# Decode turns moved, unequal MoE steps per turn, six warm-up matmuls, masks added by VectorE in later units, and six units' exponentials and sums on ScalarE

## The chip, the core and the metric

The kernel runs on one core of one Trainium2 chip. The metric is the device time of one execution in microseconds (us), and a kernel is judged by the median of its runs. The core's engines each work through their own list of instructions in order: TensorE (PE, matmuls), VectorE (DVE), ScalarE (ACT), GpSimd (POOL), and SyncE (SP), which here only issues DMAs. They wait for each other by semaphores.

## The reference

```
scores = scale * q @ k.T                  # 4 batches, 8 heads, 576 positions, 64 dims
mask: local (0 <= i-j < 32) for heads 0..3, strided (i >= j, i % 32 == j % 32) for heads 4..7
attn  = exp(scores - max) / (sum + 1e-9)
x     = attn @ v                          # -> 2304 tokens x 512
x     = (sigmoid(x @ w_gate) * (x @ w_val)) @ w_out      # MoE 1, 1536 wide
out   = softplus(x @ w_in) @ w_out2                      # MoE 2, 2048 wide
```

## The kernel before

**Two kinds of work in one stream.** The attention is cut into 32 units (8 to a batch: a pair of heads and 4 to 6 pieces of the sequence; local units have pieces of 64 queries by 96 keys, strided units of 54 by 54). The MoE layers work on blocks of 512 tokens; each "step" of theirs is three 512-column matmuls, since every operand is split into a high and a low part (`mm3`, L67 to L69). The weights come as 64-bit words, and a "decode" of one piece (128x512, `decode_steps`) makes a high and a low part of it: two VectorE instructions (L108, L112), then L117 on VectorE, L121 on ScalarE, L122 and L125 on VectorE and L126 on GpSimd. While the attention runs, 12 pieces are decoded: 6 of weight group 0 (`w00`, `w01`, `w02`: gate, value and down weights), then 6 of group 1.

**The turn.** The attention is a hand-written pipeline in turns u = 0 to 34 (`stage`). In turn u the program issues `exponent(u-1)`, `scores(u)`, `values(u-3)`, loads, the first half of a decode if u is in `decode_at`, then `normalize(u-1)`, the second half of the decode, `outputs(u-3)` and `p_transposes(u-2)`. Between these parts the loop puts MoE steps from a generator (`filler`) and, in the first 9 turns, one `keep_busy` matmul on a constant (L372). The order is fixed: nothing is rescheduled, so an engine's list is the program's order.

**One unit's way.** `scores`: a mask matmul (identity by a mask table, L422) starts the PSUM bank `ps_s`, and the score matmuls add to it (L429). VectorE reduces the maximum out of `ps_s` (L435) and subtracts it into `sm` (L436); ScalarE takes one exponential over the whole of `sm` in the next turn (L443); VectorE sums (L451) and takes the reciprocal (L452); GpSimd multiplies (L453). In the turn after that, PE transposes `sm` into `ps_p` (L467) and ScalarE copies it to `pt` (L470). In the third turn PE multiplies `pt` by v into `ps_o` (L485), ScalarE rounds it to `xh` (L505), and VectorE takes the rest into `xl` (L506). There are two `ps_s` banks, and three banks for MoE results.

**Which turn does what.** Group 0 is decoded in turns 4, 5, 9, 10, 12 and 13, group 1 in turns 18 to 23. The first window of MoE steps (24: 8 for gates, 8 for values, 8 for the down projection of token block 0) puts 2 each into turns 7, 8 and 9; the other 18 are spread evenly over turns 11 to 18 (2, 2, 2, 3, 2, 2, 2, 3). `load_next` asks for the next raw weight piece on SP's queue: one ahead of the turns, others in turns 2, 5, 6 and 7, later ones behind each decode. After the attention the rest is MoE alone, ordered by `step`, `down` and `decode_next`.

Of the kernel before, what the change touches and what calls it, by code (L numbers as in the profile page):

```python
# [8 lines left out]
F32 = mybir.dt.float32  # L9
# [3 lines left out]
AF = mybir.ActivationFunctionType  # L13
ALU = mybir.AluOpType
AX = mybir.AxisListType
# [5 lines left out]
P = 128  # L21
# [11 lines left out]
HQ = 64  # L33
# [10 lines left out]
def tile_sparse_attention_moe_moe2(  # L44
# [10 lines left out]
    nc = tc.nc  # L55
    SCALE = 1.0 / float(D) ** 0.5
# [35 lines left out]
    def load_next():  # L92
        if todo:
            g, m, c = piece = todo.pop(0)
            src = w1[g, m] if g < NG1 else w2[g - NG1, m // 2]
            raw = rawp.tile([P, PIECE], U64, tag="raw", name="raw")
            nc.sync.dma_start(out=raw, in_=src[:, c * PIECE:(c + 1) * PIECE])
            raws[piece] = raw
            queue.append(piece)
# [181 lines left out]
    def attention():  # L281
        with ExitStack() as actx:
# [11 lines left out]
            pools = {  # L294
                "g": pool("gp", 1), "t": pool("tp", 2), "d": pool("decp", 1), "e": nc.vector,
                "hy": pool("ps_hy", 3, space=PSUM),
            }

            units = []
# [12 lines left out]
            qbuf = [const.tile([P, 2, QW], F32, name=f"qbuf{j}") for j in range(2)]  # L312

            def load(j, parts=1):
                b, hp, c0, cn = units[2 * j]
                loc, w, m = dims(2 * j)
                cn += units[2 * j + 1][3]
                qq = qbuf[j % 2]
                kk = qkp.tile([P, STRIDE + S], F32, tag="k", name="kt")
                k0, kn = (0, STRIDE + S) if loc else (STRIDE, cn * m)  # L320
                qn = (cn - 1) * m + HQ
                for i in range(parts):
                    for h in range(2):
                        r = slice(h * HQ, (h + 1) * HQ)
                        a, e = (0, units[0][3] * m, qn)[i:i + 2] if parts > 1 else (0, qn)
                        nc.sync.dma_start(out=qq[r, h, a:e], in_=q[b, hp][r, a:e])
                    a, e = (0, units[0][3] * m + w - m, kn)[i:i + 2] if parts > 1 else (0, kn)
                    (nc.scalar if j < 2 else nc.sync).dma_start(
                        out=kk[:, a:e], in_=k[b, hp][:, k0 + a:k0 + e]
                    )  # L330
                for i in (2 * j, 2 * j + 1):
                    qt[i], kt[i] = qq, kk

# [9 lines left out]
            load(1)  # L343
            load_v(0)
            load_v(1)
            load_next()
            load_v(2)

            scratch = acc[NBA - 1]
            ident = scratch[:, 0:P]  # L350
            make_identity(nc, ident)
            nc.vector.memset(qbuf[0][HQ:2 * HQ, 0, :], 0.0)
            nc.vector.memset(qbuf[0][0:HQ, 1, :], 0.0)

            one = const.tile([P, P], F32R, name="one")
            nc.vector.tensor_copy(one, ident)
# [5 lines left out]

            for t in sbuf:
                nc.vector.memset(t[:, :, LK:], 1e-9)
            for t in qbuf[1:]:
                nc.vector.memset(t[HQ:2 * HQ, 0, :], 0.0)
                nc.vector.memset(t[0:HQ, 1, :], 0.0)

            def keep_busy(n):
                ps = bank(pools, "y", "ps_w")  # L370
                for _ in range(n):
                    nc.tensor.matmul(ps, lhsT=one, rhs=idle, start=True, stop=True)  # L372
# [29 lines left out]
            def mask_runs(i):  # L402
                b, hp, c0, cn = units[i]
                if hp >= NLP:
                    return [(0, cn, m_str)]
                first, rest = m_loc[:, 0:LK], m_loc[:, LK:2 * LK]
                return [(0, 1, first), (1, cn, rest)] if c0 == 0 else [(0, cn, rest)]

            sm, pts, outs = {}, {}, {}

            def scores(i):
                b, hp, c0, cn = units[i]
                loc, w, m = dims(i)
                qq, kk = qt.pop(i), kt.pop(i)
                s = sbuf[i % 3][:, 0:cn, LK - w:LK]
                st = smp.tile([P, 2, 6], F32, tag="st", name="st")
                sm[i] = (s, sbuf[i % 3][:, 0:cn, LK - w:], st)
                ps = ps_s.tile([P, TB], F32, tag="s", name="ps_s")
                pv = ps[:, 0:cn * w].rearrange("p (c w) -> p c w", c=cn)
                runs = mask_runs(i)  # L420
                for j, (a0, a1, t) in enumerate(runs):
                    nc.tensor.matmul(  # L422
                        pv[:, a0:a1, :], lhsT=one,
                        rhs=t.unsqueeze(1).to_broadcast([P, a1 - a0, w]),
                        start=(j == 0), stop=False,
                    )
                for c in range(cn):
                    for h in range(2):
                        nc.tensor.matmul(  # L429
                            pv[h * HQ:(h + 1) * HQ, c, :],  # L430
                            lhsT=qq[:, h, (c0 + c) * m:(c0 + c) * m + HQ],
                            rhs=kk[:, (c0 + c) * m:(c0 + c) * m + w], start=False, stop=(c == cn - 1),
                        )
                top = st[:, 0, 0:cn]
                nc.vector.tensor_reduce(out=top, in_=pv, axis=AX.X, op=ALU.max)  # L435
                nc.vector.tensor_tensor(  # L436
                    out=s, in0=pv, in1=top.unsqueeze(2).to_broadcast([P, cn, w]), op=ALU.subtract
                )

            def exponent(i):  # L440
                m2 = 2 * HQ
                s = sm[i][0]
                nc.scalar.activation(out=s[:m2], in_=s[:m2], func=AF.Exp, scale=SCALE)  # L443

            def normalize(i):
                cn = units[i][3]
                loc, w, m = dims(i)
                m2 = 2 * HQ
                s, more, st = sm[i]
                r = st[:m2, 1, 0:cn]  # L450
                nc.vector.tensor_reduce(out=r, in_=more, axis=AX.X, op=ALU.add)  # L451
                nc.vector.reciprocal(r, r)  # L452
                nc.gpsimd.tensor_tensor(  # L453
                    out=s[:m2], in0=s[:m2], in1=r.unsqueeze(2).to_broadcast([m2, cn, w]),
                    op=ALU.mult,
                )
# [54 lines left out]
            PB = 2 * NPAIR  # L511
            START = PB + SKEW

            def stage(u):
                dec = decode_steps(pools, u >= PB) if u in decode_at else iter(())
                if 0 <= u - 1 < NU:
                    exponent(u - 1)
                if u < NU:
                    scores(u)
                if u % 2 and u + 3 < NU:  # L520
                    load((u + 3) // 2)
                if 0 <= u - 3 < NU:
                    values(u - 3)
                if 3 <= u < NU:
                    load_v(u)
                if u in (2, 5, 6, 7):
                    load_next()
                next(dec, None)
                yield
                if 0 <= u - 1 < NU:  # L530
                    normalize(u - 1)
                next(dec, None)
                if 0 <= u - 3 < NU:
                    outputs(u - 3)
                yield
                if 0 <= u - 2 < NU:
                    yield from p_transposes(u - 2)
# [11 lines left out]
                    yield from step((0, 2), (1, 2), pools)  # L549

            ahead = {START - 4: 2, START - 3: 2, START - 2: 2}
            units_of = [3 * GC * NCC, 8 * GC * NCC, 6 * GC * NCC]
            units_of[0] -= sum(ahead.values())
            filler = window(0)
            decode_at = (4, 5, 9, 10, 12, 13) + tuple(range(18, 24))
            keep_busy(3)
            for u in range(NU + SKEW):
                t, pos = divmod(u - START, PB)
                if t > 0 and pos == 0:
                    for _ in filler:  # L560
                        pass
                    filler = window(t)
                fill = ahead.get(u, 0)
                if t >= 0:
                    total = units_of[t]
                    fill = (pos + 1) * total // PB - pos * total // PB
                n = 0
                for j, _ in enumerate(stage(u)):
                    if u < START - 2 and j == 1:
                        keep_busy(1)  # L570
                    while n < fill * (j + 1) // 4:
                        n += 1
                        next(filler, None)
                while n < fill:
                    n += 1
                    next(filler, None)
# [3 lines left out]
    with tc.manual_schedule():  # L580
        attention()

        late = ctx.enter_context(tc.tile_pool(name="late", bufs=1))
# [9 lines left out]
        for i, cur in enumerate(rest):  # L593
            g, t = cur
# [91 lines left out]
```

## Time and profile before

| | us |
|---|---|
| median of 3 runs (949.97 to 950.58) | 950.56 |
| the profiled execution's own time | 950.28 |
| its span, first to last instruction | 948.5 |
| PE busy in the span | 931.4 |
| VectorE busy | 601.8 |
| ScalarE busy | 383.9 |
| GpSimd busy | 229.3 |

The span is what the trace shows; 1.8 us of the execution's time lie around it. PE is busy for 98% of the span, so a look at shares alone does not tell where time may be had: one has to look for the stretches in which PE waits, or runs at a lower granted clock.

### The profile page before, as it was taken

Reading aid. Unit: us, or ns where it says so; the run is one execution under the profiler, and the core shown is the slowest. Engines: PE = TensorE matmul, PEld = TensorE weight load, DVE = VectorE, ACT = ScalarE, POOL = GpSimd, SP = SyncE. Lnnn points to the kernel's source line nnn. Section 1 sums busy time; section 2 is a strip of 40 time slices with the busy share of each in tenths; the row PEclk is TensorE's granted clock in tenths of the full one; section 3 lists DMA queues with packets and bytes.
Section 4 is the critical chain, followed back from the end, with each engine's and each line's share of the span. In section 5 each row is a group of like instructions: output and inputs, shape, how many; then the busy total and the mean of one; then the engine's idle time right before and its main releaser. Section 6 shows DMA issues by size and latency. Waiting matters only on the chain.

```text
span 948.5 us, 13659 instructions
## 1 busy us (share of the span) xinstructions
PE 931.4 (98%) x5476; PEld 776.3 (82%) x5476; DVE 601.8 (63%) x979; ACT 383.9 (40%) x693; POOL 229.3 (24%) x194
## 2 busy tenths in 40 slices
PE   7889999999999999999999999999999999999998
PEld 5667888789888888888888887888888888888886
DVE  7787765337567367457555467676767685858554
ACT  2455545524122112112123355454545554545443
POOL 3232211004224023122125442221313040403000
PEclk9889999999999999999999999999999999999999
DMA  8655332002112011011110011110101020200022
GB/s 226 186 159 154 122 101 61 17 1 89 45 45 81 8 45 67 23 45 46 45 37 30 22 45 45 36 53 23 67 23 66 6 85 1 82 8 23 0 89 112
DMA packets 20688, 57.44 MB, mean 61 GB/s; under 512 B 2704, under 2 KB 3216, under 8 KB 20624
## 3 DMA queue, kind: packets, MB, share of 16 engines
q1 hardware_dynamic: 20192, 55.94, 18.3%
q8 instruction: 43, 0.70, 0.3%
q10 hardware_dynamic: 432, 0.62, 0.2%
q14 instruction: 21, 0.17, 0.1%
HBM read 51.83 MB, written 4.72 MB: 60 GB/s over the span
## 4 chain that ended last, share of the span: by engine, by line
PE 92%; DVE 5%; ACT 1%; POOL 1%; issue 1%; POOLq 0%; DVEq 0%
PE ps_y L67 12%; PE ps_y L69 12%; PE ps_y L68 12%; PE ps_h L69 7%; PE ps_h L68 7%; PE ps_h L67 7%; PE ps_g L67 5%; PE ps_g L68 5%; PE ps_g L69 5%; PE ps_v L67 5%; PE ps_v L69 5%; PE ps_v L68 5%; PE ps_s L429 2%; PE ps_o L485 2%; PE ps_p L467 1%; DVE f L112 1%
## 5 line engine op out<-in xcount | busy, mean ns | idle before, releaser
L156 ACT ACTIVATE gh<-sg 128x512 fp32r<-128x512 f32 (+1 forms) x140 | 82.5, 589 | 255.0 <-DVE sg L189 183.8
L157 DVE TENSOR_TENSOR gl<-sg,gh 128x512 fp32r<-128x512 f32 (+1 forms) x140 | 98.7, 705 | 50.2 <-ACT gh L156 46.6
L260 DVE TENSOR_TENSOR acc<-ps_y,acc 128x512 f32<-128x512 f32 x126 | 86.6, 688 | 68.4 <-PE ps_y L69 66.8
L209 DVE TENSOR_TENSOR acc<-ps_y,acc 128x512 f32<-128x512 f32 (+1 forms) x100 | 61.5, 634 | 68.7 <-PE ps_y L69 68.6
L240 DVE SCALAR_TENSOR_TENSOR sg<-ps_h,sg 128x512 f32<-128x512 f32 (+1 forms) x80 | 50.5, 632 | 37.2 <-ACT sg L233 37.1
L189 DVE TENSOR_TENSOR sg<-ps_v,sg 128x512 f32<-128x512 f32 (+1 forms) x60 | 38.2, 636 | 56.2 <-PE ps_v L69 56.1
L231 ACT ACTIVATE sg<-ps_h 128x512 f32<-128x512 f32 (+1 forms) x80 | 43.8, 548 | 61.2 <-PE ps_h L69 61.2
L112 DVE SCALAR_TENSOR_TENSOR f<-raw,f 128x512 uint32<-128x512 uint32 x68 | 66.4, 977 | 2.3
L125 POOL TENSOR_TENSOR f<-f,w00h 128x512 f32<-128x512 f32 x12 | 18.5, 1544 | 184.6 <-ACT w00h L121 184.6
L68 PE MATMUL ps_h<-xl,w00h 128*128 128x512 f32 (+1 forms) x160 | 58.9, 368 | 0.0
L69 PE MATMUL ps_h<-xh,w00l 128*128 128x512 f32 (+1 forms) x160 | 58.8, 368 | 0.0
L69 PE MATMUL ps_h<-xh,w10l 128*128 128x512 f32 (+1 forms) x160 | 58.8, 368 | 0.0
L68 PE MATMUL ps_h<-xl,w10h 128*128 128x512 f32 (+1 forms) x160 | 58.8, 368 | 0.0
L67 PE MATMUL ps_h<-xh,w00h 128*128 128x512 f32 (+1 forms) x160 | 58.8, 368 | 0.0
L67 PE MATMUL ps_h<-xh,w10h 128*128 128x512 f32 (+1 forms) x160 | 58.8, 368 | 0.0
L67 PE MATMUL ps_y<-w02h,gh 128*128 128x512 f32 x144 | 56.2, 391 | 0.6 <-ACT gh L156 0.6
L68 PE MATMUL ps_y<-w02l,gh 128*128 128x512 f32 x144 | 56.1, 390 | 0.0
L67 PE MATMUL ps_y<-w12h,gh 128*128 128x512 f32 x144 | 56.1, 390 | 0.0
L69 PE MATMUL ps_y<-w02h,gl 128*128 128x512 f32 x144 | 56.1, 390 | 0.0
L68 PE MATMUL ps_y<-w12l,gh 128*128 128x512 f32 x144 | 56.1, 390 | 0.0
L69 PE MATMUL ps_y<-w12h,gl 128*128 128x512 f32 x144 | 56.1, 390 | 0.0
L453 POOL TENSOR_TENSOR sm<-sm,st 128x480 f32<-128x480 f32 (+3 forms) x32 | 25.6, 799 | 123.9 <-DVE st L452 85.7
(121 smaller groups left out, 2420.6 us busy)
## 6 DMA issues: line engine op xcount, KB each, us to landing
raw<-in_w_dram SPq DMA_DIRECT2D x68, 512.0 KB, 3.4
out_dram<-acc SPq DMA_DIRECT2D x18, 256.0 KB, 2.0
qbuf<-in_q_dram SPq DMA_DIRECT2D x16, 151.0 KB, 3.5
kt<-in_k_dram SPq DMA_DIRECT2D x8, 297.0 KB, 4.0
qbuf<-in_q_dram SPq DMA_DIRECT2D x14, 144.0 KB, 3.6
vt<-in_vl_dram SPq DMA_DIRECT2D x8, 240.0 KB, 3.1
kt<-in_k_dram SPq DMA_DIRECT2D x6, 304.0 KB, 4.2
vt<-in_vl_dram SPq DMA_DIRECT2D x8, 192.0 KB, 3.8
```

What stands on the lines that cost most here:

```text
L67: nc.tensor.matmul(ps, lhsT=lh, rhs=rh, start=first, stop=False)
L68: nc.tensor.matmul(ps, lhsT=lh, rhs=rl, start=False, stop=False)
L69: nc.tensor.matmul(ps, lhsT=ll, rhs=rh, start=False, stop=last)
L112: nc.vector.scalar_tensor_tensor(out=f, in0=high, scalar=0xC0000000, in1=f, op0=ALU.bitwise_and, op1=ALU.bitwise_or,)
L156: nc.scalar.activation(out=gh[:, c, 0:n], in_=src, func=AF.Copy)
L157: nc.vector.tensor_tensor(out=gl[:, c, 0:n], in0=src, in1=gh[:, c, 0:n].bitcast(F32), op=ALU.subtract)
L189: nc.vector.tensor_tensor(out=sg, in0=ps[:, 0:n], in1=sg, op=ALU.mult)
L209: nc.vector.tensor_tensor(out=y, in0=ps[:, 0:n], in1=y, op=ALU.add)
L231: nc.scalar.activation(out=sg, in_=ps, func=AF.Abs)
L240: nc.vector.scalar_tensor_tensor(out=sg, in0=ps, scalar=0.0, in1=sg, op0=ALU.max, op1=ALU.add)
L260: nc.vector.tensor_tensor(out=y, in0=ps, in1=y, op=ALU.add)
L453: nc.gpsimd.tensor_tensor(out=s[:m2], in0=s[:m2], in1=r.unsqueeze(2).to_broadcast([m2, cn, w]), op=ALU.mult,)
```

## The change

- **Decode turns.** Group 0 is decoded in turns 1, 4, 7, 8, 11 and 12. `load_next` is called once inside the first `load` (ahead of the second unit pair's queries and the first v pieces in SP's list), and in turns 2, 4, 5 and 7; the refill behind a decode begins with turn 7.
- **Steps per turn.** The 18 MoE steps of turns 11 to 18 become 5, 5, 1, 1, 1, 1, 1, 3.
- **Warm-up.** Six `keep_busy` matmuls ahead of turn 0 in place of three, and two in place of one in a decode turn among the first 9 turns (1, 4, 7, 8). The zeroing of the first q buffer on VectorE moves behind the constants that the warm-up needs.
- **Late mask.** From unit 20 on the mask matmul is gone; VectorE adds the mask table to the scores from PSUM into `sm`, and maximum and subtraction read `sm`. That is one more VectorE instruction per unit, two in units 24 and 26.
- **Six units by ScalarE** (`by_act`: 1, 4, 7, 8, 11, 12, the decode turns). VectorE takes only the negated maximum; ScalarE scales it (one copy of 128x4 to 128x6), and in the next turn takes the exponential piece by piece straight from `ps_s`, with the maximum as bias and the sum as accumulator output: 30 instructions of 128x96 or 128x54 in place of 6 whole ones. VectorE's subtraction and sum are gone for these units; it adds 1e-9 to the sums. `ps_s` is held until ScalarE has read it, a turn later.

```diff
+                    if parts > 1 and i == 1:
+                        load_next()
...
-            nc.vector.memset(qbuf[0][HQ:2 * HQ, 0, :], 0.0)
-            nc.vector.memset(qbuf[0][0:HQ, 1, :], 0.0)
...
+            by_act = (1, 4, 7, 8, 11, 12)
...
-                runs = mask_runs(i)
+                late = i >= 2 * PB + PB // 2
+                runs = [] if late else mask_runs(i)
...
+                if late:
+                    for a0, a1, t in mask_runs(i):
+                        nc.vector.tensor_tensor(
+                            out=s[:, a0:a1], in0=pv[:, a0:a1], op=ALU.add,
+                            in1=t.bitcast(F32).unsqueeze(1).to_broadcast([P, a1 - a0, w]),
+                        )
+                    pv = s
                 top = st[:, 0, 0:cn]
+                if i in by_act:
+                    nc.vector.tensor_reduce(out=top, in_=pv, axis=AX.X, op=ALU.max, negate=True)
+                    nc.scalar.activation(out=top, in_=top, func=AF.Copy, scale=SCALE)
+                    raw_s[i] = pv
+                    return
...
+                if i in by_act:
+                    pv = raw_s.pop(i)
+                    for c in range(units[i][3]):
+                        nc.scalar.activation(
+                            out=s[:, c, :], in_=pv[:, c, :], func=AF.Exp, scale=SCALE,
+                            bias=st[:, 0, c:c + 1], accum_out=st[:, 1, c:c + 1],
+                        )
+                    return
...
+                if i in by_act:
+                    nc.vector.tensor_scalar_add(r, r, 1e-9)
+                else:
+                    nc.vector.tensor_reduce(out=r, in_=more, axis=AX.X, op=ALU.add)
...
-                if u in (2, 5, 6, 7):
+                if u in (2, 4, 5, 7):
...
+            first_fill = (5, 5, 1, 1, 1, 1, 1, 3)
...
-            decode_at = (4, 5, 9, 10, 12, 13) + tuple(range(18, 24))
-            keep_busy(3)
+            decode_at = (1, 4, 7, 8, 11, 12) + tuple(range(18, 24))
+            keep_busy(6)
...
-                if t >= 0:
+                if t == 0:
+                    fill = first_fill[pos]
+                elif t > 0:
...
-                        keep_busy(1)
+                        keep_busy(2 if u in decode_at else 1)
```

VectorE's list from the maximum of unit 1 (turn 1) on, before: `ps_s` are the scores, `sm_92` to `sm_94` the three softmax buffers, `st` the maxima and sums.

```order
L435 TENSOR_REDUCE st<-ps_s 128x4
L436 TENSOR_TENSOR sm_93<-ps_s,st 128x4x96
L451 TENSOR_REDUCE st<-sm_92 128x5
L452 RECIPROCAL st<-st 128x5
L435 TENSOR_REDUCE st<-ps_s 128x5
L436 TENSOR_TENSOR sm_94<-ps_s,st 128x5x96
L451 TENSOR_REDUCE st<-sm_93 128x4
L452 RECIPROCAL st<-st 128x4
```

The same place after; `raw` is the undecoded weight piece.

```order
L445 TENSOR_REDUCE st<-ps_s 128x4
L108 TENSOR_SCALAR f<-raw 128x512
L112 SCALAR_TENSOR_TENSOR f<-raw,f 128x512
L476 TENSOR_REDUCE st<-sm_92 128x5
L477 RECIPROCAL st<-st 128x5
L117 TENSOR_SCALAR e<-f 128x512
L122 SCALAR_TENSOR_TENSOR e<-raw,e 128x512
L125 TENSOR_TENSOR f<-f,w00h 128x512
L449 TENSOR_REDUCE st<-ps_s 128x5
L450 TENSOR_TENSOR sm_94<-ps_s,st 128x5x96
L474 TENSOR_SCALAR st<-st 128x4
L477 RECIPROCAL st<-st 128x4
```

The first decode now stands in turn 1, between the maximum of unit 1 and the sum of unit 0; the subtraction and the sum of unit 1 are gone.

ScalarE's list from turn 12 into turn 13, after: `sg` and `gh` are the gated values of a MoE step and their high part, `L460` the exponentials by piece of units 11 (`sm_94`) and 12 (`sm_92`).

```order
L460 ACT_TABLE_LOAD
L460 ACTIVATE sm_94,st<-ps_s,st 128x96 x4
L446 ACTIVATE st<-st 128x6
L156 ACTIVATE gh<-sg 128x512
L121 ACTIVATE w02h<-f 128x512
L530 ACTIVATE xh<-ps_o 128x256
L495 ACTIVATE pt<-ps_p 96x384
L495 ACTIVATE pt<-ps_p 96x256
L156 ACTIVATE gh<-sg 128x512
L460 ACTIVATE sm_92,st<-ps_s,st 128x54 x6
L530 ACTIVATE xh<-ps_o 128x320
```

Both `L156` now stand in turn 12, one of them ahead of the exponentials of unit 12, which are the last readers of that unit's `ps_s`.

## Rows read from the trace of the kernel before

**Rows 1.** PE's waits over the whole span: total us, times, longest.

```profile
PE ps_o L485 <- ACT pt L470: 6.6, 5, 2.4
PE ps_w L372 <- DVE w12l L358: 2.8, 1, 2.8
```

**Rows 2.** Busy time by stretch; columns: PE, PEld, DVE, ACT, POOL, granted clock, DMA.

```profile
4.83:15.71 10.88, 9.77 (x111) 7.55 (x112) 6.22 (x13) 2.82 (x6) 2.66 (x6) 1.00 0.94 258
15.71:28.71 13.00, 10.21 (x145) 8.04 (x142) 12.33 (x27) 5.37 (x15) 5.08 (x5) 0.76 0.63 184
28.71:44.94 16.23, 15.50 (x214) 12.61 (x212) 11.28 (x24) 6.88 (x16) 3.79 (x5) 0.99 0.63 189
33.02:37.47 4.45, 4.45 (x56) 3.69 (x55) 2.35 (x5) 1.74 (x6) 0.64 (x1) 1.00 0.79 245
44.94:53.63 8.69, 5.67 (x50) 4.21 (x48) 7.41 (x15) 5.17 (x10) 3.58 (x4) 0.77 0.61 188
53.63:72.21 18.58, 16.88 (x216) 13.51 (x215) 15.10 (x33) 8.93 (x19) 5.27 (x6) 0.92 0.52 161
93.00:180.00 87.00, 87.00 (x811) 70.18 (x810) 53.95 (x106) 44.75 (x82) 15.77 (x17) 1.00 0.28 86
```

**Rows 3.** The chain that ended last, 4.83 to 72.21 us, by line.

```profile
by line: PE ps_s L429 12.7%; DVE e L122 9.0%; PE ps_p L467 6.7%; DVE f L112 6.2%; DVE st L451 5.6%; DVE st L435 5.2%; PE ps_o L485 4.8%; DVE f L125 4.5%; issue 4.2%; PE ps_w L372 4.1%; DVE sm L436 4.0%; PE ps_s L422 3.7%; DVE xl L506 3.7%; 
```

**Rows 4.** VectorE's timeline: start, us, instruction, [idle before it].

```profile
9.62 0.56 DVE L435 TENSOR_REDUCE st<-ps_s 128x4 f32<-128x384 f32 x1 [0.55 <-PE ps_s L429]
...
17.00 0.50 DVE L435 TENSOR_REDUCE st<-ps_s 128x6 f32<-128x324 f32 x1
17.60 0.50 DVE L436 TENSOR_TENSOR sm<-ps_s,st 128x324 f32<-128x324 f32 x1
18.01 0.42 DVE L108 TENSOR_SCALAR f<-raw 128x512 uint32<-128x512 uint32 x1
...
19.07 0.55 DVE L451 TENSOR_REDUCE st<-sm 128x4 f32<-128x388 f32 x1
...
19.75 0.40 DVE L117 TENSOR_SCALAR e<-f 128x512 uint32<-128x512 uint32 x1
...
21.90 0.41 DVE L506 TENSOR_TENSOR xl<-ps_o,xh 128x256 fp32r<-128x256 f32 x1
...
72.10 0.69 DVE L189 TENSOR_TENSOR sg<-ps_v,sg 128x512 f32<-128x512 f32 x1
73.48 0.69 DVE L157 TENSOR_TENSOR gl<-sg,gh 128x512 fp32r<-128x512 f32 x1 [0.70 <-ACT gh L156]
```

**Rows 5.** PE's timeline: a MoE step, a wait, and the mask matmuls of two turns.

```profile
39.39 0.50 PE L67 MATMUL ps_g<-xh,w00h 128*128 128x512 f32 x1
...
40.19 0.71 PE L467 MATMUL ps_p<-one,sm 128*54 128x128 f32 x5
...
48.62 0.80 PE L485 MATMUL ps_o<-pt,vt 96*64 96x64 f32 x20 [2.45 <-ACT pt L470]
...
72.21 0.45 PE L422 MATMUL ps_s<-m_loc,one 128*128 128x96 f32 x2
72.59 1.05 PE L429 MATMUL ps_s<-kt,qbuf 128*64 128x96 f32 x20
...
101.23 0.29 PE L422 MATMUL ps_s<-m_str,one 128*128 128x270 f32 x1
101.44 0.79 PE L429 MATMUL ps_s<-kt,qbuf 128*64 128x54 f32 x20
```

**Rows 6.** ScalarE's groups by shape to 72.2 us: busy us, mean ns.

```profile
L443 ACT ACTIVATE sm<-sm 128x480 f32<-128x480 f32 x4 | 2.4, 598 | 5.7 <-DVE sm L436 5.7
L443 ACT ACTIVATE sm<-sm 128x270 f32<-128x270 f32 x3 | 1.3, 422 | 0.0
```

**Rows 7.** The raw weight pieces of the first 30 us, issue to landing.

```profile
DMA to landing us min/median/max: 3.8/5.0/6.1
```

**Rows 8.** SyncE's queue from the start.

```profile
0.73 3.76 SPq L326 DMA_DIRECT2D qbuf<-in_q_dram  x6
```

More of the change, by code (lines that the diff above doesn't have):

```diff
@@ L345, in attention @@
             load_v(1)
-            load_next()
             load_v(2)
@@ L364, in attention @@
                 nc.vector.memset(t[:, :, LK:], 1e-9)
-            for t in qbuf[1:]:
+            for t in qbuf:
                 nc.vector.memset(t[HQ:2 * HQ, 0, :], 0.0)
@@ L407, in mask_runs @@
                 return [(0, 1, first), (1, cn, rest)] if c0 == 0 else [(0, cn, rest)]
-            sm, pts, outs = {}, {}, {}
+            sm, pts, outs, raw_s = {}, {}, {}, {}
+            by_act = (1, 4, 7, 8, 11, 12)
             def scores(i):
@@ L431, in scores @@
                             lhsT=qq[:, h, (c0 + c) * m:(c0 + c) * m + HQ],
-                            rhs=kk[:, (c0 + c) * m:(c0 + c) * m + w], start=False, stop=(c == cn - 1),
-                        )
-                top = st[:, 0, 0:cn]
+                            rhs=kk[:, (c0 + c) * m:(c0 + c) * m + w],
+                            start=late, stop=(late or c == cn - 1),
+                        )
+                if late:
[5 more added lines that the diff above has]
+                    pv = s
+                top = st[:, 0, 0:cn]
+                if i in by_act:
[3 more added lines that the diff above has]
+                    return
                 nc.vector.tensor_reduce(out=top, in_=pv, axis=AX.X, op=ALU.max)
@@ L441, in exponent @@
                 m2 = 2 * HQ
-                s = sm[i][0]
+                s, _, st = sm[i]
+                if i in by_act:
[6 more added lines that the diff above has]
+                    return
                 nc.scalar.activation(out=s[:m2], in_=s[:m2], func=AF.Exp, scale=SCALE)
@@ L450, in normalize @@
                 r = st[:m2, 1, 0:cn]
-                nc.vector.tensor_reduce(out=r, in_=more, axis=AX.X, op=ALU.add)
+                if i in by_act:
+                    nc.vector.tensor_scalar_add(r, r, 1e-9)
+                else:
+                    nc.vector.tensor_reduce(out=r, in_=more, axis=AX.X, op=ALU.add)
                 nc.vector.reciprocal(r, r)
@@ L514, in stage @@
             def stage(u):
-                dec = decode_steps(pools, u >= PB) if u in decode_at else iter(())
+                dec = decode_steps(pools, u > 6) if u in decode_at else iter(())
                 if 0 <= u - 1 < NU:
```

## The prediction

> **What bounds the kernel now.** PE is busy for 931.4 of 948.5 us, so time can only come from the 17 us in which it does not work, from its slow stretches, or from work taken off its list. I read the stretches first. From 93 to 180 us PE is busy for 87.00 of 87.00 us at granted clock 1.00 [rows 2]; what goes on there and later is a full list of matmuls. The slack lies in the first 72 us. Turns 0 to 15, from the first mask matmul at 4.83 to that of turn 16 at 72.21 [rows 2, 5], take 67.4 us, and the five stretches that cover them hold 9.77 + 10.21 + 15.50 + 5.67 + 16.88 = 58.0 us of busy PE [rows 2]: 9.4 us idle. Of the busy time part runs at a reduced clock. Busy time times the missing share is 10.21 x 0.24 + 15.50 x 0.01 + 5.67 x 0.23 + 16.88 x 0.08 = 5.3 us [rows 2].
>
> Next, who is waited for. PE's largest wait is that of the value matmuls for `pt`, 6.6 us in five times, and 2.8 us pass before the first warm-up [rows 1]. ScalarE is the engine named, but it has little to do; the chain of waits shows what it waited for. On the chain of 4.83 to 72.21 us stand L122, L112 and L125, the decode on VectorE, with 9.0, 6.2 and 4.5% [rows 3]. The order explains it: ScalarE's decode copy (L121) stands ahead of the `pt` copies in its list and needs L112. A late L112 makes `pt` late, and PE stands: 2.45 us in turn 11 [rows 5]. In the decode turns 4 to 6 VectorE is busy 12.33 of 13.00 us; before them it is busy for only 6.22 of 10.88, and in turn 8, which has no decode, for 2.35 of 4.45 [rows 2]. So the six decodes lie unevenly, and this is the bound of the early part.
>
> **VectorE, turns 1 to 8.** One decode turn in steps from start to start [rows 4]: maximum 0.60 (17.00 to 17.60), subtraction 0.41, first half of the decode 1.06 (18.01 to 19.07), sum and reciprocal 0.68 (19.07 to 19.75), second half 2.15 (19.75 to 21.90), `xl` some 0.35. That is 5.2 us, 3.2 of them decode. In a `by_act` unit the subtraction is gone in its turn and the sum in the next; a tiny add comes instead, which no row shows. Between nothing and a whole sum (0.55) I take 0.15, as it has a column for each piece, like the reciprocal in the 0.68. Six units save 6 x (0.45 + 0.55 - 0.15) = 5 us of VectorE. Walking the new order with these steps (up to 0.2 longer for the wide local shapes and the strided `xl`) turns 1 to 8 need 4.6, 1.5, 2.4, 4.8, 1.7, 1.9, 5.1 and 4.7: 26.7 us. Turn 1's maximum starts at 9.62 [rows 4]; I put it at 9.9, because the four memsets now stand ahead of the mask table's cast and hold PE's first mask up by some 0.6, while the warm-up starts earlier. VectorE is through turn 8 at 36.6, with four pieces decoded. In the old order turn 11 begins at 44.94 with the fourth decode still running in it.
>
> **PE, turns 7 to 16.** Turn 8 takes 4.45 us when PE is not held up [rows 2]; a second warm-up adds 0.3 (a MoE step of three such matmuls takes 0.80, 39.39 to 40.19 [rows 5]; I take 0.75 where steps follow each other). From a start of turn 7 at 26.0, when the sums of turn 6 are through VectorE and GpSimd, turns 7 and 8 end at 35.5, in step with VectorE. Turn 9 has no warm-up, 3.9; turn 10 no MoE step, 2.6: turn 11 starts at 42.0, 2.9 us earlier than now. Its list is 2.6 of attention and five steps of 0.75, 6.3 us, and the 2.45 us wait [rows 5] is gone, since L112 no longer comes late. Turn 12 is 2.2 + 3.75, ending at 54.2; turn 13 2.2 + 0.75, ending at 57.2.
>
> **The new wait.** Turn 12 is the heaviest of VectorE: maximum 0.6, decode 3.2, twice product, wait for ScalarE and rest of a gated value (72.10 to 74.1, 2.0 each with the 0.70 wait [rows 4]), 0.6 of others: 8.4 us from 49.3 to 57.7. The second product ends some 1.4 earlier, ScalarE's copy takes 0.6, and only then come the six exponentials of unit 12, which hold its score bank. PE's scores of turn 14 want that bank. So ScalarE's price per piece decides. No row shows an exponential of 54 or 96 columns with a bias from memory and a sum. From 598 ns for 480 columns and 422 for 270 [rows 6] a piece would be 0.25 to 0.29; that is the low end, and twice that, 0.55, the high end, for a sum that has to be brought out. I take 0.4: the six end at 56.9 + 2.4 = 59.3, PE waits 2.1 us, and what is queued behind (values, transposes, the step) waits too. Turns 14 and 15, 3.1 each, put turn 16 at 65.4 in place of 72.2. Two MoE steps more are done by then (19 against 17), worth 1.5. Early gain 6.8 + 1.5 = 8.3; I take 0.5 off for a clock that falls in turns 4 to 6, where PE still idles, and is slow into turn 7: 7.8.
>
> The Trainium skill ("ScalarE: Activation LUTs", What ACT_TABLE_LOAD costs) gives 280 ns + 0.833 per column for an activation with a bias from memory, and an overlap of 93 ns between neighbours. By that rule a piece would be an estimated 0.23 to 0.27 us, the wait in turn 14 about 1.1, and the time 938.4. It says nothing of the price of the sum, and no row here shows either.
>
> **The late masks.** 12 units lose a mask matmul. From the mask's start to the first score matmul it is 0.38 for 96 + 384 columns and 0.21 for 270 [rows 5]; with 0.27 and 0.24 between these for 384 and 324 columns, 8 strided units give 1.8 and 4 local ones 1.3: 3.1 us off a list that has no gap. VectorE gets 14 additions, as long as the subtraction (0.50 [rows 4]) or somewhat longer, some 7 us. They are hidden in the 87.0 - 53.95 = 33 us that VectorE is idle from 93 to 180 [rows 2], where these 12 turns lie. Without that cover they would cost up to 7.
>
> **DMA.** The first raw piece is issued fifth on SP's queue; six issues take 3.76 from 0.73 [rows 8], so at about 3.2. Landing takes 3.8 to 6.1 [rows 7]: 7.0 to 9.3, ahead of L108 at 10.5. Behind it the second unit pair's queries come up to 2 us later, still before turn 2. Nothing is charged.
>
> **Sum.** The profiled execution took 950.28 (0.03% from the median): 950.28 - 7.8 - 3.1 = 939.4.
>
> **Rivals.**
> 1. The clock falls as it does now, in the early turns and again at the new wait. Rows 2 speak for it (0.76 and 0.77 in the stretches where PE idled); the added warm-ups and the shorter waits against. All 5.3 us stay instead of 0.5: 944.2.
> 2. Only the masks pay: waits I do not see take back the early part, as an in-order VectorE standing at L108 for the raw piece (an arrival at 12 costs 1.5 in turns 1 to 8), or the order `xh`, `pt` behind a fourth decode. About 947.
> 3. The walk is too careful and PE is never held up: 58.0 - 5.3 of work, plus 1.2 of warm-ups and 1.5 of steps, from 5.4: turn 16 at 60.8, gain 12.9 + 3.1: 934.3.
> 4. Slower: ScalarE's 30 pieces. VectorE waits in order at its add for the accumulated sums, so each unit's 4 to 6 pieces have a window of some 2.5 us, 15 in all. They outgrow everything saved when 30c - 15 = 2.1 + 11, at c = 0.94 us apiece, over twice the 0.42 of a whole 270-column one [rows 6]. At 1.05 it would be 953.
>
> **How the numbers follow.** Chances: my sum within 936.5 to 942 0.55, rival 1 with 942 to 945.5 0.17, rival 3 0.10, rival 2 0.12, rival 4 0.03, no change otherwise 0.03. The range runs from rival 3's bound, 934.5, to 945.5, where the full clock loss and a piece at 0.55 (0.9 more) meet; it leaves out 2 and 4 and a tail of 3, under 0.2. About 0.2% (1.9 us) is what a measurement here can tell from no change. Faster than 948.7 are the sum and rivals 1 and 3 whole, rival 2 nearly: 0.93; same 0.04; slower 0.03.
>
> **What would show it.** Right: turn 11's first mask near 42, turn 16's near 65; no wait of values for `pt` over 1 us in turns 8 to 13; a wait of scores for ScalarE in turn 14; no PE idle from 90 to 180 and 3 us less in that stretch. Wrong: VectorE idle at L108 in turn 1, pieces over 0.55 us, or a clock under 0.8 after 45 us.

## The result, and the profile after

| | before | after |
|---|---|---|
| median of 4 runs, us | 950.57 (949.97 to 953.34) | 939.85 (938.20 to 940.98) |
| the profiled execution, us | 950.28 | 940.98 |
| its span, us | 948.5 | 939.2 |

The ratio is 0.9876, 95% interval [0.9858, 0.9893]: faster, by 10.7 us in the medians and 9.3 in the two profiled executions. A second set of five runs of the changed kernel gave 941.36 (940.71 to 942.92), ratio 0.9902 [0.9889, 0.9915]. The forecast was 939.4 in 934.5 to 945.5. The changed kernel's nine runs spread over 4.7 us and those of the kernel before, taken beside all the experiments, over 4.6 (949.95 to 954.56), so small differences below are read from stretches of the traces and not from medians alone.

The page of the changed kernel, busy time by engine and the granted clock in 40 slices:

```profile
PE 927.2 (99%) x5469; PEld 772.7 (82%) x5469; DVE 602.6 (64%) x987; ACT 390.3 (42%) x753; POOL 229.5 (24%) x194
PEclk9999999999999999999999999999999999999999
```

PE is busy for 4.2 us less and idle for 5.1 us less (12.0 in place of 17.1). PE's waits in the changed kernel (total us, times, longest), beside [rows 1]:

```profile
PE ps_w L371 <- DVE w12l L357: 2.0, 1, 2.0
PE ps_s L423 <- DVE sm L450: 1.9, 1, 1.9
PE ps_s L430 <- DMA qbuf<-in_q_dram: 1.5, 1, 1.5
PE ps_p L492 <- POOL sm L478: 1.3, 2, 1.0
...
PE ps_o L510 <- ACT pt L495: 0.4, 1, 0.4
```

The wait that led the list, value matmuls for ScalarE's `pt`, fell from 6.6 to 0.4 us. Two new ones stand there: the scores of turn 14 for their bank, 1.9, and the scores of turn 2 for their queries, 1.5.

PE's timeline in the changed kernel, the first matmul of the scores of turns 7, 11, 12, 13, 14 and 16, and what follows that of turn 14:

```profile
26.57 0.38 PE L423 MATMUL ps_s<-m_str,one 128*128 128x270 f32 x1
...
42.20 0.42 PE L423 MATMUL ps_s<-m_loc,one 128*128 128x384 f32 x1
...
47.95 0.31 PE L423 MATMUL ps_s<-m_str,one 128*128 128x324 f32 x1
...
53.63 0.29 PE L423 MATMUL ps_s<-m_str,one 128*128 128x270 f32 x1
...
58.58 0.45 PE L423 MATMUL ps_s<-m_str,one 128*128 128x324 f32 x1 [1.88 <-DVE sm L450]
58.95 1.53 PE L430 MATMUL ps_s<-kt,qbuf 128*64 128x54 f32 x24
...
66.12 0.45 PE L423 MATMUL ps_s<-m_loc,one 128*128 128x96 f32 x2
```

Turn 16 begins at 66.12 in place of 72.21 [rows 5], with two MoE steps more behind it. Where both kernels have the same work behind them, at the scores of turn 19, PE is at 85.72 before and 77.83 after: 7.9 us. The rest is made in the units with late masks. Busy time by stretch in the changed kernel (columns as in [rows 2]): the scores of turn 2 to the middle of turn 6, turns 13 to 15, and the scores of unit 19 to those of unit 31:

```profile
15.00:28.00 13.00, 11.32 (x212) 9.25 (x209) 11.48 (x29) 8.19 (x30) 6.37 (x7) 1.00 0.86 263
...
54.00:66.00 12.00, 10.12 (x150) 8.29 (x149) 8.01 (x20) 6.67 (x25) 2.85 (x5) 0.86 0.53 139
77.83:165.93 88.10, 87.90 (x801) 69.69 (x800) 63.13 (x123) 47.29 (x87) 17.88 (x19) 1.00 0.33 98
```

The last stretch takes 88.10 us; the same work took 89.53 before (85.72 to 175.25 us). So the late masks bring 1.4 us, and 7.9 + 1.4 = 9.3 is the whole difference of the spans. The clock that stood at 0.76 in turns 4 to 6 [rows 2] is 1.00 there now, and 0.86 in turns 13 to 15: the score matmuls of turn 14 take 1.53 us, where 24 of that form take 0.91 at the full clock. The granted clock from 58.95 to 60.28 us is 0.50, the lower of the two levels, 1.2 GHz, after PE had stood still for 1.88 us.

### The profile page after: what moved, and what is told of

It reads as the page before. It is cut to its first block, busy times and chain, and to the rows that moved or that the text cites. A ratio compares the mean times of both kernels' runs of the same rounds, so it can differ in the third digit from the quotient of the medians.

```text
span 939.2 us, 13729 instructions
## 1 busy us (share of the span) xinstructions
PE 927.2 (99%) x5469; PEld 772.7 (82%) x5469; DVE 602.6 (64%) x987; ACT 390.3 (42%) x753; POOL 229.5 (24%) x194
## 4 chain that ended last, share of the span: by engine, by line
PE 92%; DVE 4%; ACT 1%; DMA 1%; issue 1%; SPq 0%; POOL 0%; DVEq 0%; ACTq 0%; POOLq 0%
PE ps_y L67 12%; PE ps_y L69 12%; PE ps_y L68 12%; PE ps_h L67 7%; PE ps_h L69 7%; PE ps_h L68 7%; PE ps_g L67 5%; PE ps_g L69 5%; PE ps_g L68 5%; PE ps_v L67 5%; PE ps_v L69 5%; PE ps_v L68 5%; PE ps_s L430 2%; PE ps_o L510 2%; PE ps_p L492 2%; DMA raw<-in_w_dram 1%
## 5 line engine op out<-in xcount | busy, mean ns | idle before, releaser
L156 ACT ACTIVATE gh<-sg 128x512 fp32r<-128x512 f32 (+1 forms) x140 | 82.5, 589 | 254.2 <-DVE sg L189 183.1
L112 DVE SCALAR_TENSOR_TENSOR f<-raw,f 128x512 uint32<-128x512 uint32 x68 | 66.4, 977 | 2.3
L122 DVE SCALAR_TENSOR_TENSOR e<-raw,e 128x512 f32<-128x512 uint32 x68 | 53.0, 780 | 2.4
```

The lines of the kernel that those rows point to most:

```text
L112: nc.vector.scalar_tensor_tensor(out=f, in0=high, scalar=0xC0000000, in1=f, op0=ALU.bitwise_and, op1=ALU.bitwise_or,)
L122: nc.vector.scalar_tensor_tensor(out=ef, in0=low, scalar=2.0 ** -52, in1=ef, op0=ALU.mult, op1=ALU.mult)
L156: nc.scalar.activation(out=gh[:, c, 0:n], in_=src, func=AF.Copy)
```

## The experiments

Each kernel is the changed kernel with one edit, unless it is said otherwise, and times are medians beside the kernel before on the same chip.

**x0, the changed kernel again.** No edit.

> The changed kernel once more, beside the variants on the same chip: 938 to 941 us, some 10 to 11 us under the kernel before. Its four runs so far lie 2.8 us apart. If that spread comes from the clock that falls after the wait of turn 14, or from when the first weight piece lands, the profile of another run shows one of the two differently.

Measured: 941.36, ratio 0.9902, just above the range expected. The wait ahead of turn 14 (1.9) and the slow turn 14 behind it are there again; turn 16's mask stands within 0.3 us of the first profile. Of the spread a part lies at the very start: over all profiles with six warm-ups the scores of turn 1 begin between 7.2 and 8.7 us, and the twenty score matmuls of turn 0 take from 1.05 us (x8) to 1.87 (x11). The granted clock from 5 to 8 us is 1.00 in both of these profiles, so what slows them is not shown.

**x1, masks by matmul again.**

```diff
-                late = i >= 2 * PB + PB // 2
+                late = False
```

> All masks by matmul again, the rest of the change kept. The prediction's term (3.1 us, from the mask's start to the first score matmul): 3.1 slower than the changed kernel, about 943. Theory from the trace after: units 20 to 31 now take 88.1 us in place of 89.5, so a mask matmul is worth only its columns at 2.4 GHz, and the masks 1.4: about 941.3. Rival: VectorE's 14 additions cost PE nothing and gain nothing: 939.9.

Measured: 940.80 (940.60 to 942.21), ratio 0.9897, which no median tells from x0. In this run turn 14 kept its clock (1.00 from 54 to 66 us), so it was 1.5 us ahead by turn 15 and lost that in the units with masks. The medians settle nothing; x11 asks again.

**x2, no unit by ScalarE.**

```diff
-            by_act = (1, 4, 7, 8, 11, 12)
+            by_act = ()
```

> No unit's exponentials by piece on ScalarE: VectorE subtracts and sums for all, 5 us more of it over turns 1 to 13. Theory (VectorE sets turns 1 to 8): units 1, 4 and 7 put 0.8 us each on those turns and 0.6 lies in turn 8, so turn 9 starts some 2.5 us later; the wait of scores for ScalarE in turn 14 goes (1.9 us and the slow clock behind it): net 0 to 2 us slower, 940 to 942. Rival (by_act is what carries the change): 4 us slower or more, 944. Rival (the pieces cost as much as they save): 938 or faster.

Measured: 942.87, ratio 0.9918 [0.9904, 0.9932]; 1.5 us over x0. Against x0's profile the scores come 1.3 us later in turns 7 and 9, 2.1 in turns 10 and 13, then only 1.0 in turn 14, since the wait for the bank is gone, and 1.5 in turn 31. As the first theory says: the 5 us that VectorE saves are worth some 2 where VectorE sets the pace, and ScalarE gives 1 of it back in turn 14.

**x3, unit 12 whole.**

```diff
-            by_act = (1, 4, 7, 8, 11, 12)
+            by_act = (1, 4, 7, 8, 11)
```

> Only unit 12 back to one whole exponential and VectorE's subtraction and sum. Theory (ScalarE's six pieces behind the second gated value hold the score bank that turn 14 wants): the wait of 1.9 us ahead of turn 14 goes, and the slow clock behind it, for 0.9 us more on VectorE in turns 12 and 13: 1 to 2 us faster, 938 to 939. Rival (as the trace labels that wait, VectorE's subtraction of unit 13 is the releaser, and VectorE is late): the wait stays or grows, 940 to 941.

Measured: 940.52 (939.43 to 941.55), ratio 0.9896. The wait of the scores of turn 14 is gone, so it was ScalarE's six exponentials that held the bank. It was not the VectorE instruction that the trace names: PE now starts these scores while that instruction (L450 of unit 13, at 57.84) is still to come. Only part of the gain is there, though: from the first mask of turn 11 to that of turn 16 this kernel takes 23.10 us, the changed kernel 23.92 and 23.95 (x0). PE's and VectorE's timelines around turn 14 of this kernel:

```profile
56.38 0.31 PE L423 MATMUL ps_s<-m_str,one 128*128 128x324 f32 x1
...
57.84 0.44 DVE L450 TENSOR_TENSOR sm<-ps_s,st 128x270 f32<-128x270 f32 x1
...
60.21 0.84 PE L492 MATMUL ps_p<-one,sm 128*54 128x128 f32 x6 [1.68 <-POOL sm L478]
```

PE now waits 1.68 us a little later, for GpSimd's multiply of unit 12, whose sum VectorE takes late. Both theories are half right: ScalarE holds the bank, and behind it VectorE is late in any case.

**x4, even steps.**

```diff
-            first_fill = (5, 5, 1, 1, 1, 1, 1, 3)
+            first_fill = (2, 2, 2, 3, 2, 2, 2, 3)
```

> The 18 MoE steps of turns 11 to 18 spread evenly again (2, 2, 2, 3, 2, 2, 2, 3), the rest kept. Theory (VectorE's load of turn 12 with two gated values and a decode makes the wait ahead of turn 14): the wait of turn 14 goes, but PE idles some 1 to 2 us in turns 11 and 12, where VectorE needs 5.0 and 4.4 us and PE's list is 4.1 and 3.7: 0 to 1 us slower than the changed kernel, 940 to 942. Rival (the unequal steps are what hides the decodes): 3 us slower, 944.

Measured: 940.10, ratio 0.9878, no difference. The wait of turn 14 is gone, and PE idles earlier instead. Turns 11 and 12 of this kernel:

```profile
45.00:54.00 9.00, 7.19 (x96) 5.74 (x94) 7.22 (x15) 8.95 (x31) 3.19 (x4) 0.81 0.47 150
```

PE is busy 7.19 of 9.00 us at 0.81; in the changed kernel it is busy for all of this stretch. ScalarE, at 8.95 of 9.00, sets the pace here: two table loads, 10 exponentials by piece, the sigmoids and a decode copy fall together. The unequal steps cover that with MoE work and pay the same amount at turn 14: from the scores of turn 11 to those of turn 19, with the same work done, it is 35.4 us here and 35.3 in the changed kernel.

**x5, the old warm-ups.**

```diff
-            keep_busy(6)
+            keep_busy(3)
...
-                        keep_busy(2 if u in decode_at else 1)
+                        keep_busy(1)
```

> Three warm-ups and one per turn again, the rest kept. Theory (VectorE sets turns 1 to 6 and the warm-ups only fill PE's idle time): the granted clock of turns 4 to 6 falls to about 0.5 as in the kernel before, which costs little where PE waits anyhow, and turns 7 and 8 are 0.3 shorter each: within 1 us of the changed kernel. Rival (the warm-ups hold the clock and that is worth time): turns 6 to 8 slow, 2 to 3 us slower, 943.

Measured: 940.17 (939.18 to 942.39), ratio 0.9875 [0.9851, 0.9898]: no difference. The clock from 16 to 28 us is 1.00 here too (the profile is of the slowest of the four runs), so the fall to 0.5 that was expected did not come, and it is not the warm-ups that hold the clock. PE idles for 1.9 of these 12 us, against 2.8 in the kernel before; but x10 idles for 3.1 of them at 1.00, so shorter waits do not explain it either.

**x6, the old decode turns.**

```diff
-            decode_at = (1, 4, 7, 8, 11, 12) + tuple(range(18, 24))
+            decode_at = (4, 5, 9, 10, 12, 13) + tuple(range(18, 24))
...
-                dec = decode_steps(pools, u > 6) if u in decode_at else iter(())
+                dec = decode_steps(pools, u >= PB) if u in decode_at else iter(())
...
-                if u in (2, 4, 5, 7):
+                if u in (2, 5, 6, 7):
```

The first `load_next` goes back behind the second v piece as well; the units by ScalarE stay 1, 4, 7, 8, 11 and 12.

> Decode turns 4, 5, 9, 10, 12 and 13 again, with the loads that went with them; by_act, steps per turn, warm-ups and late masks kept. Theory (the place of the decodes carries the gain): VectorE is idle again in turns 1 and 2, is the bound in 4 to 6 and 9 to 10, ScalarE's copies for the value matmuls come late again and PE waits for them over 2 us in turn 11: 5 us slower than the changed kernel, 945 to 947. Rival (by_act and the unequal steps carry it): within 1.5 us, 942.

Measured: 951.78 (948.72 to 953.26, 10 runs), ratio 0.9995 [0.9980, 1.0011]: the whole gain is gone, more than the theory said. PE's waits, and the one in turn 11:

```profile
PE ps_o L509 <- ACT pt L494: 6.3, 4, 2.4
...
49.75 0.80 PE L509 MATMUL ps_o<-pt,vt 96*64 96x64 f32 x20 [2.44 <-ACT pt L494]
```

This is the kernel before's wait [rows 1, 5], to 0.01 us in turn 11. The clock has fallen as well: it is 0.88 from the first mask to the scores of turn 19, against 0.92 in the kernel before. From the scores of unit 19 to those of unit 31 it is 88.09 us, so what the late masks bring is still there, and the early turns are slower than before. Here the units by ScalarE no longer coincide with the decodes, and the five steps of turns 11 and 12 need weights decoded just before them, so more than the place of the decodes is upset.

**x7, v pieces later.**

```diff
-            load_v(0)
-            load_v(1)
-            load_v(2)
...
+                if u == 1:
+                    for i in range(3):
+                        load_v(i)
```

> The first three v pieces are asked for in turn 1 behind the third pair's loads, not ahead of the turns, so that the first weight piece and the second pair's queries share the DMA engines with less. Theory (those two land late because of the v pieces): VectorE's 0.7 us at L108 and PE's 1.5 us at the scores of turn 2 shrink, and turn 7 starts some 0.7 us earlier: 0.5 to 1 faster, 940. Rival (hidden, or the v pieces now come late for turn 3): the same or slower.

Measured: 940.86, ratio 0.9885, no difference. VectorE's wait at the first L108 is gone (0.3 us come at the second) and so is PE's for the queries, but a wait of 0.8 for the first v piece came in turn 3, and turn 7 starts at 26.16, where it did in x0 (26.23). The rival holds.

**x8, one step moved from turn 12 to 13.**

```diff
-            first_fill = (5, 5, 1, 1, 1, 1, 1, 3)
+            first_fill = (5, 4, 2, 1, 1, 1, 1, 3)
```

> Steps per turn 5, 4, 2, 1, 1, 1, 1, 3: the last value step, and with it the second gated value on VectorE and its copy on ScalarE, moves from turn 12 to turn 13, behind the exponentials of unit 12. Theory (turn 12 asks 8.4 us of VectorE, 2 of them for that value, and this makes the wait ahead of turn 14 whoever is named as the releaser): the wait of 1.9 us goes and no other takes its place, the clock stays at 1.00 from 54 to 66 us: turn 16 starts 2 to 3 us earlier, 938 to 939. Rival (as with unit 12 taken whole, the wait moves on to GpSimd's multiply or to the down projection): under 1 us, 940 to 941.

Measured: 938.39 (937.48 to 939.16), ratio 0.9859 [0.9838, 0.9880], the fastest kernel of the study, 3.0 us under x0, and 1.8 and 2.5 under x5 and x7, which have the steps 5, 5 and ran on the same chip as this one. Turns 13 to 15 of this kernel, by stretch and in PE's timeline:

```profile
54.00:66.00 12.00, 10.74 (x160) 8.80 (x161) 8.91 (x22) 6.57 (x21) 3.39 (x4) 1.00 0.68 187
...
56.01 0.31 PE L423 MATMUL ps_s<-m_str,one 128*128 128x324 f32 x1
56.25 0.91 PE L430 MATMUL ps_s<-kt,qbuf 128*64 128x54 f32 x24
58.42 0.69 PE L510 MATMUL ps_o<-pt,vt 96*64 96x64 f32 x16 [1.26 <-ACT pt L495]
```

The scores of turn 14 do not wait, the clock stays at 1.00, and 1.26 us of wait are left for `pt`. Turn 16's scores begin 2.4 us earlier than in x0; from the first mask of turn 11 to that of turn 16 it is 21.78 us in place of 23.95, so 2.2 of it come from these turns. That is what turn 14 cost: the wait and the slow clock behind it, less this rest. In x1, with the steps 5, 5 and the wait but the full clock in turn 14, the same stretch takes 22.43, so some 1.5 of the 2.2 are the clock.

**x9, the same steps, two v pieces later.** The edit of x8, and `load_v(1)` and `load_v(2)` moved into turn 1.

> The same steps per turn, and the second and third v pieces asked for in turn 1 behind the third pair's loads, the first one still ahead of the turns. Theory: PE's wait for the second pair's queries in turn 2 (up to 1.5 us) goes and nothing comes late for turn 3, but VectorE still sets turns 1 to 8, so at most 0.5 us better than the steps alone. Rival (DMA order matters more): 1.5 better.

Measured: 938.70 (938.09 to 939.56), ratio 0.9862. No wait for queries or v pieces is left, and nothing is gained: VectorE sets turns 1 to 8, as the theory has it.

**x10, the kernel before with the new decode turns alone.** The reverse of x6's edit, put on the kernel before.

> The kernel before with nothing but the decode turns 1, 4, 7, 8, 11 and 12 and the loads that go with them. With the decode turns put back the whole gain was gone; if their place carries it by itself, most of the early part is here already: VectorE has 5 us more to do than in the changed kernel and PE one late mask per unit more, so some 3 us short of it: 943 to 945. Rival (the parts need each other, unequal steps and by_act above all): 947 or slower.

Measured: 944.86 (944.44 to 945.43), ratio 0.9929 [0.9904, 0.9954]: 5.9 us faster than the kernel before, by this one part. PE's longest waits in it:

```profile
PE ps_o L486 <- ACT pt L471: 4.4, 3, 2.5
PE ps_p L468 <- POOL sm L454: 3.2, 3, 1.7
```

With all softmax work left on VectorE, `pt` and GpSimd's multiplies still come late: the waits for `pt` fell from 6.6 to 4.4 us, those for GpSimd rose from 1.3 to 3.2. What went is the low clock. From the first mask matmul to the scores of turn 19, first the kernel before, then this one, then the changed kernel (columns as in [rows 2]):

```profile
4.83:85.72 80.89, 71.36 (x888) 56.54 (x888) 61.84 (x128) 36.49 (x82) 22.53 (x28) 0.92 0.62 182
```

```profile
4.84:79.90 75.06, 66.79 (x888) 53.22 (x889) 61.72 (x128) 36.49 (x82) 22.56 (x28) 1.00 0.67 196
```

```profile
5.01:77.83 72.82, 67.46 (x892) 54.41 (x892) 57.00 (x122) 43.23 (x142) 22.41 (x28) 0.98 0.74 202
```

Of the 5.8 us that the new decode turns bring here, 4.6 are busy time: the same 888 matmuls, at clock 1.00 in place of 0.92. PE's idle time fell only from 9.5 to 8.3 us. The four runs of this kernel have a mean granted clock of 0.998 or 0.999 over the whole execution, the eight of the kernel before beside them 0.989 to 0.996. Why the clock holds while PE idles almost as long, no run shows. The other parts of the change then take the idle time from 8.3 to 5.4.

**x11, x8 with masks by matmul.** The edits of x8 and x1 together.

> Steps per turn 5, 4, 2, 1, 1, 1, 1, 3 with all masks by matmul: the value of the late masks where no slow clock of turn 14 blurs it. Theory (a mask matmul is worth its columns at 2.4 GHz, 0.11 to 0.20 us, as the stretch of units 20 to 31 says): 1.4 slower than the same steps with late masks, about 939.8, and units 20 to 31 take 89.5 us in place of 88.1. The prediction's term: 3.1 slower, 941.5. Rival: no difference, 938.4.

Measured: 940.66 (939.73 to 941.49), ratio 0.9882; 2.3 us over x8, between the two theories, with ranges of 1.7 us each. The stretch from the scores of unit 19 to those of unit 31 tells more, first x11, then x8:

```profile
76.41:165.93 89.52, 89.48 (x814) 72.19 (x814) 57.60 (x111) 47.44 (x87) 17.89 (x19) 1.00 0.33 97
```

```profile
75.16:163.26 88.10, 87.90 (x801) 69.68 (x800) 63.15 (x123) 47.31 (x87) 17.85 (x19) 1.00 0.33 98
```

It is 1.4 us, as in the first pair of traces. The other difference between the two profiles, 1.2 us at the scores of turn 19, stands already at the scores of turn 1 (8.7 against 7.2 us), where the two kernels are the same: it is the start, not the masks.

## Why the prediction was right, point by point

**VectorE, turns 1 to 8: right.** VectorE was predicted to be through turn 8 at 36.6 and was at 37.15, the start of the next maximum. The first decode did run in turn 1. Its L108 waited, though, which the prediction had excluded and had named as a sign of being wrong. Turn 1's maximum, that L108, and the maximum behind turn 8:

```profile
9.20 0.56 DVE L445 TENSOR_REDUCE st<-ps_s 128x4 f32<-128x384 f32 x1
...
10.48 0.43 DVE L108 TENSOR_SCALAR f<-raw 128x512 uint32<-128x512 uint32 x1 [0.72 <-DMA raw<-in_w_dram]
...
37.15 0.55 DVE L449 TENSOR_REDUCE st<-ps_s 128x4 f32<-128x384 f32 x1
```

The raw piece was issued at 3.25 as estimated, but took 7.2 us to land, not 3.8 to 6.1 [rows 7], and the second pair's queries, issued behind it, came late for turn 2 (1.5 us of PE's time). "Nothing is charged" was wrong by the 0.7 us; the PE wait lay beside VectorE's work, as x7 and x9 show. That the walk still ends within 0.6 us is partly luck: it began at 9.20, not at 9.9. The first mask came 0.2 us later than before (5.01 against 4.83), not 0.6, and the scores of turn 1 began earlier than before (8.24 against 8.66). VectorE also stood 0.9 us for PE's scores in turns 4 and 7.

**PE, turns 7 to 16: right in the starts, the cause only in part.** Predicted starts of turns 11, 12, 13, 14 and 16: 42.0, 48.3, 54.2, 59.3, 65.4; measured 42.20, 47.95, 53.63, 58.58, 66.12. The cause given, that a late L112 holds ScalarE's `pt` copies, is there in the kernel before. Ahead of PE's wait of 2.45 us in turn 11 ScalarE's list reads:

```profile
47.12 0.63 ACT L121 ACTIVATE w01h<-f 128x512 fp32r<-128x512 f32 x1 [3.93 <-DVE f L112]
...
48.05 0.78 ACT L470 ACTIVATE pt<-ps_p 96x384 f32<-96x384 f32 x2
```

With the decode turns put back, that wait returns (2.44, x6). But the larger part of what the new decode turns bring is not this wait: in x10 4.6 of 5.8 us are the clock. The prediction has that part in its sum, since it keeps 0.5 of the 5.3 us of reduced clock. The reasons that it gave against rival 1, added warm-ups and shorter waits, are not what decides: x10 has the old warm-ups and nearly the old idle time, and its clock is 1.00. That the clock holds in the early turns was forecast rightly, and its reason stays open.

**The new wait: right in place and cause, its price off.** ScalarE at the end of turn 12 and the pieces of unit 12 (the first, the second and the last of six):

```profile
56.25 0.63 ACT L156 ACTIVATE gh<-sg 128x512 fp32r<-128x512 f32 x1 [2.70 <-DVE sg L189]
56.79 0.29 ACT L460 ACTIVATE sm<-ps_s,st 128x54 f32<-128x54 f32 x1
56.98 0.19 ACT L460 ACTIVATION_READ_ACCUMULATOR sm<-ps_s,st 128x1 f32 x1
57.07 0.30 ACT L460 ACTIVATE sm<-ps_s,st 128x54 f32<-128x54 f32 x1
...
58.19 0.32 ACT L460 ACTIVATE sm<-ps_s,st 128x54 f32<-128x54 f32 x1
58.38 0.22 ACT L460 ACTIVATION_READ_ACCUMULATOR sm<-ps_s,st 128x1 f32 x1
```

A piece takes 0.28 us from start to start (0.31 for 96 columns), not 0.4: an exponential, and a second instruction that reads the sum. By the rule of the Trainium skill ("ScalarE: Activation LUTs", What ACT_TABLE_LOAD costs) it would be an estimated 0.23 and 0.27 without that instruction; the measurement decides. PE waited 1.88 us, 2.1 predicted, and that they agree is luck: the pieces ended 0.7 us earlier than predicted (58.6, not 59.3) and PE came 0.5 us earlier (56.7, not 57.2). The trace names VectorE's L450, which ended at 58.43; x3, in which this unit alone is taken whole again, shows that ScalarE's pieces hold the bank. What the prediction did not charge is the clock behind this wait: turn 14 took 4.5 us, not 3.1, at a granted clock of 0.62, under the 0.8 that it had named as a sign of being wrong. It charged 0.5 us for turns 4 to 6 instead, where the clock stayed at 1.00.

**The late masks: the term that was mis-sized.** 3.1 us were predicted, 1.4 measured. The mechanism holds: VectorE's additions are hidden (63.13 us busy in 88.10, PE idle for 0.2). The size took the whole distance from the mask's start to the first score matmul as the mask's. PE's timeline at the scores of unit 21, before (its mask and scores are in [rows 5]) and after:

```profile
100.99 0.40 PE L69 MATMUL ps_v<-xh,w01l 128*128 128x512 f32 x1
...
102.07 0.76 PE L485 MATMUL ps_o<-pt,vt 96*64 96x64 f32 x20
```

```profile
92.96 0.40 PE L69 MATMUL ps_v<-xh,w01l 128*128 128x512 f32 x1
93.29 0.79 PE L430 MATMUL ps_s<-kt,qbuf 128*64 128x54 f32 x20
94.10 0.80 PE L510 MATMUL ps_o<-pt,vt 96*64 96x64 f32 x20
```

From the MoE matmul to the first score matmul it is 0.33 us; with the mask between it was 0.24 (100.99 to 101.23) + 0.21 [rows 5] = 0.45. Only 0.12 is saved, about the 270 columns at 2.4 GHz (0.113, an estimate of one column per cycle), and some 0.1 that the prediction put down to the mask is a gap ahead of the score matmuls that stays. Over the 12 units these distances fall from 5.96 to 3.93 us: 2.0 saved, not 3.1. Another 0.6 is lost behind the scores, most of it in units 21 and 22, where the value matmuls follow the first score matmul after 0.81 and 1.05 us in place of 0.63 and 0.74; in unit 22 the trace has them waiting 0.3 us for ScalarE's `pt`. That leaves 1.4.

**The sum.** For the profiled execution 7.8 + 3.1 = 10.9 was predicted, 7.9 + 1.4 = 9.3 came. That the early part is right to 0.1 us is partly luck: a clock that fell and a landing that came late, neither charged where it fell, stand against pieces that were dearer in the sum than on the chip and against a walk that began earlier. Rival 1 (the clock) came true for turn 14 in four of the five profiles that have its wait (x1 is the fifth), and in x0 also at the start: 0.50 from 12 to 14 us, behind the wait for the queries. Three slips of the prediction's arithmetic change nothing: the line through [rows 6] gives 0.24 to 0.28 for a piece, the full clock loss and a piece at 0.55 meet at 945.1, and rival 4 at 1.05 us apiece comes to 953.7.

**How the parts share the gain.** New decode turns alone bring 5.9 us (x10), most of it by a clock that stays up; everything else without them brings nothing (x6). The units by ScalarE are worth 1.5 (x2), the masks 1.4; the unequal steps as they stand (x4) and the warm-ups (x5) nothing that can be measured, though steps of 5, 4, 2 would be worth some 2 more (x8: 2.2 in the traces, 1.8 to 3.0 in the medians).

## What to carry to other kernels

When several engines take turns in a hand-written order, look for an earlier stretch in which the engine that is waited for has idle time (here VectorE, busy for only 6.22 of 10.88 us) and move work there; the wait itself may be three instructions away, in another engine's list. When a step is taken out of an engine's list, its neighbours still stand some way apart: what is saved is the distance between them before less the distance after, not the distance from the step to the next instruction. And when work is packed into one turn, price every buffer whose last reader comes behind it: one step moved by one turn (x8) gave 2.2 us in the traces, more than the units by ScalarE (1.5) or the late masks (1.4). Last, ask of each gain whether idle time went or the same instructions ran faster: in x10 it was mostly the second, and the waits alone would not have told.

## What the runs showed of the hardware

- ScalarE's activation with a sum is two instructions: 0.31 us (54 columns) or 0.34 (96), and 0.21 for the read of the sum; they overlap with their neighbours, so that a pair costs 0.28 or 0.31.
- After a table load of 1.28 us ScalarE's next activation began at once (44.42 + 1.28 = 45.70; the sigmoid starts at 45.71).
- A 512 KB load took between 4.3 and 7.2 us to land in the first 30 us of the changed kernel, and 3.8 to 6.1 in the kernel before. Those issued at 3.25, 11.5 and 23.9 us took 7.2, 7.0 and 7.0, so a long landing is not confined to the first transfers.
- The same 888 matmuls took 71.36 us at a mean granted clock of 0.92 (the kernel before) and 66.79 at 1.00 (x10), with 9.5 and 8.3 us of idle time between them.
- After the same wait of 1.88 us in turn 14 the clock fell at once in the first profile of the changed kernel (scores 1.53 us in place of 0.91), in the middle of the turn in x0 (six transposes 1.48 us against 0.84), and not at all in x1 (1.89): turn 14 took 4.5, 4.4 and 3.0 us. So executions whose lists are the same up to there differ in this by 1.5 us.
